# Loading wq in two transfers: sixteen rows first, then the other 112

## The chip, the cores and the metric

The kernel runs on one core of a Trainium2 chip. The metric is device time in microseconds for one execution. Six kinds of engine matter here: TensorE (PE, matrix products), VectorE (DVE), ScalarE (ACT), GpSimd (POOL), SyncE (SP, which here only issues transfers) and the sixteen DMA engines of the core, which move data from device memory (HBM) into the on-chip memory (SBUF, 128 rows called partitions).

## The reference

One decode step of a block with two branches, mixed by a scalar gate, all in float32:

```python
g = sigmoid((x * gate_w).sum(-1))                 # x: 1 x 1 x 512
q = (x @ wq).reshape(32 heads, 128)               # wq: 512 x 4096
scores = q . k_cache * 128 ** -0.5                # k_cache, v_cache: 8 heads x 32768 x 128
a = (softmax(scores) . v_cache).reshape(4096) @ wo     # four query heads share one k/v head
b = (silu(x @ w1) * (x @ w3)) @ w2                # 512 -> 1792 -> 512
out = g * a + (1 - g) * b
```

The two caches are 134 MB each; all inputs together are 296 MB, read once.

## The kernel before, in words

The program is written out by hand. `Program.add` takes one operation for one engine with the names of what it reads and writes, and works out from these names which semaphores the engine must wait for; `emit` then writes every engine's list in the order of adding.

All bulk transfers are added with `load` (its transfer is line 194 of the profile) on the queue of SyncE. SyncE works through its list in order: it waits until the buffer of the next load is free, issues it and goes on. Each load gets one of nine semaphores in turn (`lanes`), and a load waits for the one nine places before it. Value tiles are issued by a sister of `load` at line 413, on the same queue.

There are two large buffers, `big[0]` ("big_a") and `big[1]` ("big_b"), each 128 rows of 64 KB, 8.4 MB. Their halves have the names A0, A1 and B0, B1 in the bookkeeping. A key tile, a value tile or all of wq fills one buffer exactly.

The order at the start is:

- ACT issues two small transfers, x and gate_w, one row of 2 KB each, on its own queue (line 202).
- SP issues wq into `big[0]`, as one transfer of 128 rows. Row p holds rows 4p to 4p+3 of wq, 64 KB in one piece, both in HBM and in SBUF.
- SP issues the first key tile into `big[1]`.
- POOL and DVE prepare constants. TensorE turns x into a column (line 253), DVE copies it to `xp`.
- TensorE computes q from `xp` and wq (`part`, line 268: four groups of eight products, each 32 x 512), then a small product for the gate (line 279).
- SP may now issue the second key tile into `big[0]`, in place of wq.
- ACT and DVE bring q into the form in which it is used as weights (`win`, `winc`, lines 286 to 296).

After that comes a loop over sixteen key tiles (`scores`: DVE transposes pieces at line 346, TensorE multiplies them at line 330, ACT moves the part that has to leave the buffer into `aside` at line 318), four of which make up one softmax over a pair of k/v heads. Four tiles behind it run the value tiles (`values_loop`, TensorE at line 432). Key and value loads alternate on the queue. w1 and w3 are loaded on the way. At the end come the last value tiles (line 587), wo, and w2 in five pieces (products at lines 660 and 676), a copy (line 688) and the store (line 485).

Of the kernel before, what the change touches and what calls it, by code (L numbers as in the profile page):

```python
# [13 lines left out]
P = 128  # L14
# [102 lines left out]
def kernel(  # L117
# [19 lines left out]
    NC = D // P  # L137
# [18 lines left out]
    pe, dve, act, pool = (  # L156
        lambda fn, _e=e, **kw: pr.add(_e, fn, **kw) for e in ("PE", "DVE", "ACT", "POOL")
    )
    V, A, T = nc.vector, nc.scalar, nc.tensor

    def sbuf(name, *shape):
        return nc.alloc_sbuf_tensor(name, [P, *shape], F32)[:]

    big = [sbuf("big_a", 2 * R), sbuf("big_b", 2 * R)]
# [25 lines left out]
    def load(dst, src, writes, over=()):  # L190
        lanes[0] += 1
        lane = f"load{lanes[0] % 9}"
        return pr.add(
            "SP", lambda: nc.sync.dma_start(dst, src), writes=writes, over=[*over, lane], inc=lane, by=16, also=lane,  # L194
        )

    def region(b, z):
        return big[b][:, z * R:(z + 1) * R]


    for i, t in enumerate((x.rearrange("a b n -> (a b) n"), gate_w.rearrange("(o n) -> o n", o=1))):
        pr.add("ACT", lambda i=i, t=t: nc.scalar.dma_start(rows[i][0:1, :], t), writes=[f"row{i}"], inc="row", by=16)
    load(big[0], wq.rearrange("(p c) n -> p (c n)", c=NC), ["A0", "A1"])


    ident, ones, fold = sbuf("ident", P), sbuf("ones", P), sbuf("fold", 32)
# [1 line left out]
    spot, mask, xp = sbuf("spot", 16, 8), sbuf("mask", 16), sbuf("xp", NC, 32)  # L208
# [16 lines left out]
    for src, dst, view, axes in (  # L225
# [11 lines left out]
            reads=[src], writes=[dst])  # L237
# [24 lines left out]
    for c in range(NC):  # L262
        def part(c=c):
            t = region(0, c // 2)
            for b in range(2):
                for j in range(4):
                    o = ((c % 2) * HKV + 4 * b + j) * REP * DH
                    ins = T.matmul(  # L268
                        pf[b][32 * j:32 * j + 32, :], xp[:, c, :], t[:, o:o + REP * DH],
                        start=(c == 0), stop=(c == NC - 1),  # L270
                    )
            return ins
        pe(part, reads=["A0", "A1", "xp"], writes=["f0", "f1"])


    gpr, gsm = tmp[0:1, 1].rearrange("p b d -> p (b d)"), sbuf("gsm", 1)
# [5 lines left out]
        reads=["gate0"], writes=["gate1"])  # L282
# [414 lines left out]
    a, b, c, d = flips  # L697
# [67 lines left out]
```

## Time and profile before

| | |
|---|---|
| median of 3 runs | 694.1 us (693.98 to 695.0) |
| the profiled execution | 693.89 us, its span 692.1 us |
| mean granted TensorE clock | 0.802 of full speed |
| busy: PE, DVE, ACT, POOL | 56%, 53%, 19%, 0% of the span |
| read from HBM | 296.23 MB, 428 GB/s over the span |
| transfers of SP's queue | 99.1% of the time of 16 DMA engines |

The span runs from the first to the last instruction; the profiled execution's own time is 1.8 us longer. "SPq" and "ACTq" are the instruction queues of SyncE and ScalarE, where transfers are issued. A transfer's issue is short; its data moves later, in order behind what the queue already holds. In an engine row of the timeline the first number is the start in us, the second how long, and in brackets stands how long the engine was idle before and what ended that. In rows of windows, DMA share is the busy share of the sixteen DMA engines in that stretch; it can exceed 1 by a few hundredths because a packet is counted where it starts.

### The profile page before, as it was taken

The page shows a single profiled execution, that of the slowest core. Times are in us where ns is not written, and L with a number is a line of the kernel's source. Part 1 is how long each engine was busy: PE and PEld are TensorE (multiplying, and loading weights), DVE is VectorE, ACT ScalarE, POOL GpSimd, SP SyncE. Part 2 cuts the span into 40 slices and gives each one's busy share as a digit, 9 for nine tenths or more (in the row PEclk, how much of TensorE's full clock was granted, in tenths as well). Part 3 has the DMA queues.
Part 4 walks back from the last instruction along what each step waited for, and adds up shares of the span by engine and source line. Part 5 has one row for each costly group of instructions (what it writes and reads, how often), then busy time and mean ns, then how long its engine had stood idle before and what let it go on. Part 6 is the DMA issues. An engine that isn't in the chain of part 4 may idle for free. (4 is left out here: it accounts for less than half of the span.)

```text
span 692.1 us, 5789 instructions
## 1 busy us (share of the span) xinstructions
PE 388.3 (56%) x2448; PEld 95.3 (14%) x2448; DVE 370.1 (53%) x259; ACT 134.7 (19%) x113; POOL 2.8 (0%) x15
## 2 busy tenths in 40 slices
PE   1537677566473636565564646364563646564457
PEld 0101111201010101201010101101010101211112
DVE  1049998493725637493826537492816547600701
ACT  0143323222303131220303131220303031100000
POOL 1000000000000000000000000000000000000000
PEclk9969999968686966778695779788697879865789
DMA  9999999999999999999999999999999999999996
GB/s 394 444 432 424 428 424 432 449 439 432 424 432 424 443 447 432 428 428 428 432 443 443 428 428 428 428 443 447 432 424 428 428 436 439 421 451 425 422 429 287
DMA packets 6213, 296.35 MB, mean 428 GB/s; under 512 B 694, under 2 KB 698, under 8 KB 1084
## 3 DMA queue, kind: packets, MB, share of 16 engines
q1 hardware_dynamic: 6196, 296.23, 99.1%
q8 instruction: 6, 0.10, 0.1%
q14 instruction: 3, 0.02, 0.0%
q10 hardware_dynamic: 8, 0.01, 0.0%
HBM read 296.23 MB, written 0.00 MB: 428 GB/s over the span
## 5 line engine op out<-in xcount | busy, mean ns | idle before, releaser
L346 DVE STREAM_TRANSPOSE aside<-big_a 128x2048 f32<-128x2048 f32 x41 | 94.4, 2302 | 184.3 <-DMA big_a<-in_A_k_cache_dram 184.3
L330 PE MATMUL ps<-aside,winc 128*32 128x512 f32 x512 | 89.4, 776 | 168.0 <-PEq L703 167.2
L330 PE MATMUL ps<-kt,winc 128*32 128x512 f32 x512 | 89.0, 772 | 49.1 <-PEq L703 49.1
L318 ACT COPY aside<-big_a 128x6144 f32<-128x6144 f32 x14 | 74.4, 5313 | 171.2 <-DMA big_a<-in_A_k_cache_dram 171.2
L432 PE MATMUL ps<-big_b,pv 128*32 128x512 f32 x768 | 94.9, 650 | 17.4 <-PEq L703 17.4
L346 DVE STREAM_TRANSPOSE kt<-aside 128x2048 f32<-128x2048 f32 x32 | 72.7, 2273 | 0.0
L346 DVE STREAM_TRANSPOSE kt<-big_a 128x2048 f32<-128x2048 f32 x28 | 63.5, 2269 | 0.0
L330 PEld LDWEIGHTS ps<-aside,winc 128*32 128x32 f32 x512 | 13.1, 120 | 236.6 <-issue 236.6
L358 ACT COPY sb<-ps 128x512 f32<-128x512 f32 x16 | 17.1, 1071 | 136.5 <-PE ps L330 136.5
L432 PEld LDWEIGHTS ps<-big_b,pv 128*32 128x32 f32 x768 | 27.7, 119 | 85.0 <-issue 85.0
L346 DVE STREAM_TRANSPOSE aside<-aside 128x2048 f32<-128x2048 f32 x16 | 36.3, 2269 | 0.0
L587 PE MATMUL ps<-big_b,probs 128*32 128x512 f32 x128 | 19.1, 756 | 21.1 <-DMA big_b<-in_A_v_cache_dram 21.1
L330 PEld LDWEIGHTS ps<-kt,winc 128*32 128x32 f32 x512 | 13.1, 120 | 125.4 <-issue 125.4
L596 DVE TENSOR_SCALAR red<-ps,own_b 128x128 f32<-128x128 f32 x2 | 0.7, 350 | 52.7 <-PE ps L587 52.7
L324 ACT COPY winc<-win 128x128 f32<-128x128 f32 x32 | 9.8, 307 | 77.9 <-PE ps L330 77.9
L587 PE MATMUL ps<-big_a,probs 128*32 128x512 f32 x128 | 18.1, 730 | 7.6 <-DMA big_a<-in_A_v_cache_dram 7.6
L346 DVE STREAM_TRANSPOSE aside<-big_b 128x2048 f32<-128x2048 f32 x7 | 16.0, 2291 | 11.0 <-DMA big_b<-in_A_k_cache_dram 11.0
L641 PE MATMUL ps<-win,ones 128*128 128x512 f32 (+1 forms) x40 | 21.8, 631 | 0.0
L242 PE MATMUL ps<-acc 128*128 128x512 f32 x34 | 20.0, 670 | 2.5 <-POOL acc L213 1.5
L379 DVE TENSOR_REDUCE mt<-turned 128x8 f32<-128x2048 f32 x4 | 9.2, 2292 | 20.3 <-PE turned L368 20.3
L405 DVE TENSOR_REDUCE sums<-probs 128x8 f32<-128x2048 f32 x4 | 15.3, 3834 | 2.1 <-ACT probs L398 2.1
L268 PE MATMUL turned<-big_a,xp 128*32 128x512 f32 x64 | 8.6, 699 | 12.0 <-DMA big_a<-in_A_wq_dram 12.0
(94 smaller groups left out, 186.9 us busy)
## 6 DMA issues: line engine op xcount, KB each, us to landing
big_b<-in_A_v_cache_dram SPq DMA_DIRECT2D x2, 4096.0 KB, 25.8
big_b<-in_B_w_dram SPq DMA_DIRECT2D x2, 3584.0 KB, 20.8
aside<-in_A_wo_dram SPq DMA_DIRECT2D x1, 4096.0 KB, 29.4
big_a<-in_A_wo_dram SPq DMA_DIRECT2D x1, 4096.0 KB, 20.4
big_a<-in_B_w_dram SPq DMA_DIRECT2D x2, 1024.0 KB, 23.5
big_a<-in_B_w_dram SPq DMA_DIRECT2D x1, 768.0 KB, 26.0
big_a<-in_B_w_dram SPq DMA_DIRECT2D x1, 512.0 KB, 26.7
big_a<-in_B_w_dram SPq DMA_DIRECT2D x1, 256.0 KB, 26.9
```

The source lines that it names most:

```text
L242: return T.matmul(ps_s, acc[:, 0:P], acc, start=True, stop=False, skip_group_check=True)
L268: ins = T.matmul(pf[b][32 * j:32 * j + 32, :], xp[:, c, :], t[:, o:o + REP * DH], start=(c == 0), stop=(c == NC - 1),)
L318: act(lambda: A.copy(spare, src[:, :, 32:128]), reads=[key], writes=["wo"])
L324: lambda: A.copy(winc, win[:, t // 4, :, 16 - 16 * z:48 - 16 * z]),
L330: ins = T.matmul(ps_s[32 * g:32 * g + 32, :], winc[:, c, :], kt[c % 2][:, 512 * g:512 * g + 512], start=False, stop=False, skip_group_chec ...
L346: k = dve(lambda d=dst, s=src: V.transpose(d, s), reads=[key], writes=[f"kt{c % 2}"], credit="keys")
L358: lambda: A.copy(sb[:, :, :, t % 4], ps_s.rearrange("p (n i) -> p n i", i=32)),
L379: dve(lambda: V.tensor_reduce(mt[:, 0:8], turned.rearrange("p (n q) -> p q n", q=8), axis=AX.X, op=ALU.max), reads=banks, writes=["mt"])
L405: dve(lambda: V.tensor_reduce(sums[:, 8 * w:8 * w + 8].rearrange("p (u q) -> p u q", u=2), probs[:, :, 0:1024].rearrange("p u (n q) -> p u ...
L432: ins = T.matmul(ps_o[32 * t:32 * t + 32, :], pv[:, o:o + 32], big[1][:, n * P:(n + 4) * P], start=((z, g) == (0, 0)), stop=((z, g) == (1, ...
L587: ins = T.matmul(ps_o[32 * t:32 * t + 32, :], prob[u][:, o:o + 32], vt[:, n * P:(n + 4) * P], start=((e, z, g) == (0, 0, 0)), stop=((e, z, ...
L641: return T.matmul(bank[:, 0:n], ones, win.rearrange("p w c n -> p (w c n)")[:, 0:n], start=True, stop=True)
```

## The change

The transfer of wq is split by rows. The first covers rows 0 to 15 of the buffer (1 MB), the second rows 16 to 127 (7.3 MB). Both are issued by SP, one after the other, ahead of the first key tile. The first has a name of its own, "wq", for the bookkeeping, and the q product waits for both. Every later load takes the next of the nine semaphores.

```diff
-    load(big[0], wq.rearrange("(p c) n -> p (c n)", c=NC), ["A0", "A1"])
+    wqd = wq.rearrange("(p c) n -> p (c n)", c=NC)
+    load(big[0][0:16], wqd[0:16], ["wq"])
+    load(big[0][16:P], wqd[16:P], ["A0", "A1"])
...
-        pe(part, reads=["A0", "A1", "xp"], writes=["f0", "f1"])
+        pe(part, reads=["A0", "A1", "wq", "xp"], writes=["f0", "f1"])
```

Two lines are added, so line numbers behind them are higher by two in the changed kernel (the q product's matmuls stand at line 270).

## The prediction

> **What bounds the kernel now.** I read the page from the top: engine shares, the forty slices, the queue list. Then the stretches by window for the start, the chain of waits for the end, and the timeline for the first 45 us.
>
> ```profile
> span 692.1 us, 5789 instructions
> PE 388.3 (56%) x2448; PEld 95.3 (14%) x2448; DVE 370.1 (53%) x259; ACT 134.7 (19%) x113; POOL 2.8 (0%) x15
> DMA  9999999999999999999999999999999999999996
> GB/s 394 444 432 424 428 424 432 449 439 432 424 432 424 443 447 432 428 428 428 432 443 443 428 428 428 428 443 447 432 424 428 428 436 439 421 451 425 422 429 287
> q1 hardware_dynamic: 6196, 296.23, 99.1%
> ```
>
> No engine is busy for much more than half of the span; the DMA row is 9 in every slice but the last. The queue line carries most of the argument: q1 is the queue of the SP engine, all loads go through it, and its packets fill 99.1% of what sixteen DMA engines have in 692.1 us. That leaves 0.9%, 6.2 us. The next rows show where these 6.2 us are.
>
> ```profile
> core 0: us, PE busy (x) PEld busy (x) DVE busy (x) ACT busy (x) POOL busy (x), PEclk, DMA share, GB/s
> 0.00:2.00 2.00, 0.46 (x1) 0.46 (x2) 0.00 (x0) 0.22 (x1) 1.02 (x7) 1.00 0.49 165
> 2.00:12.00 10.00, 2.22 (x6) 0.59 (x5) 2.45 (x10) 1.06 (x1) 1.79 (x8) 1.00 0.94 387
> 12.00:24.00 12.00, 0.99 (x8) 0.40 (x12) 0.48 (x1) 0.00 (x0) 0.00 (x0) 1.00 1.01 437
> ...
> 120.00:240.00 120.00, 69.65 (x444) 16.13 (x444) 68.97 (x44) 28.19 (x23) 0.00 (x0) 0.77 1.00 433
> 688.00:692.00 4.00, 1.24 (x32) 0.53 (x24) 0.29 (x1) 0.00 (x0) 0.00 (x0) 0.97 0.03 10
> ```
>
> The DMA engines are half empty for the first 2 us, a little short until 12 us, empty for the last 4 us, and full between. So there is no gap later on in which a late start could be made good. What the first transfers lose is lost at the end, unless the compute was itself waiting for something else; the chain says it was not.
>
> ```profile
> 661.57 26.71 DMA big_a<-in_B_w_dram
> 688.27 0.04 issue
> 688.32 1.10 PE turned L676 x24
> 689.42 0.02 issue
> 689.44 0.29 DVE winc L688
> ```
>
> The chain ends on a transfer that was 26.71 us on its way, almost all of it behind other data; after the last landing come 1.10 us of matmuls, a copy of 0.29 us and the store. The profiled execution took 693.89 us, 1.8 more than its span; the median of the three runs is 694.1, 0.2 above it.
>
> **The unit of the sum.** One row of wq in this layout is 64 KB (four rows of 4096 floats). From the queue line, one DMA engine moves 296.23 MB / (16 x 692.1 us x 0.991) = 27.0 GB/s while busy, so one row takes one engine 2.43 us. I call that a slot. A load of 128 rows is eight slots on each of sixteen engines, 19.4 us. The timeline agrees with that:
>
> ```profile
> 0.93 0.40 SPq L194 DMA_DIRECT2D big_a<-in_A_wq_dram  x1
> 1.39 0.41 SPq L194 DMA_DIRECT2D big_b<-in_A_k_cache_dram  x1
> 23.01 8.62 PE L268 MATMUL turned<-big_a,xp 128*32 128x512 f32 x64 [12.02 <-DMA big_a<-in_A_wq_dram]
> 31.56 0.38 PE L279 MATMUL ps<-gsm,ones 1*128 1x1 f32 x2
> 31.69 0.33 SPq L194 DMA_DIRECT2D big_a<-in_A_k_cache_dram  x1
> 43.30 2.31 DVE L346 STREAM_TRANSPOSE aside<-big_b 128x2048 f32<-128x2048 f32 x1 [9.34 <-DMA big_b<-in_A_k_cache_dram]
> ```
>
> wq is used at 23.01, the first key tile at 43.30: 20.3 us apart.
>
> **The change, part by part.** *One more issue on SP.* The wq issue takes 0.40 us; a second one pushes the first key load from 1.39 to about 1.8. Cost nothing: that load stands behind wq's 19.4 us of data anyhow. Without that cover it would be 0.4 us.
>
> *One more completion.* Another transfer posts its own completion on each engine. The page counts them with the small packets:
>
> ```profile
> DMA packets 6213, 296.35 MB, mean 428 GB/s; under 512 B 694, under 2 KB 698, under 8 KB 1084
> ```
>
> All 694 together cannot cost more than the 6.2 us that are not data, so 16 more cost at most 0.14 us. I take nothing.
>
> *One more wait on TensorE.* The q product (line 268) now waits for two landings. Queued behind it on TensorE are its own 64 matmuls, the gate product of line 279 and the whole loop; and the second key load on SP waits for line 279, since it overwrites wq's buffer. The first piece lands before the second, so the wait itself is free. If wq as a whole lands late by d, the second key load is issued at 31.69 + d, and the first key tile, behind wq on every engine, lands at about 43.30 + d. The 11.6 us between them, in which the queue still has work, stay as they are. No new hole, but no gain either.
>
> *The waits for loads nine places back* move by one number. The loads they name landed long before; cost nothing. The x and gate rows on ACT's queue pass between wq's packets and may come later than before:
>
> ```profile
> 10.38 0.61 PE L253 MATMUL ps<-ident,probs 1*128 1x1 f32 x4 [6.76 <-DMA probs<-in_gate_w_dram]
> ```
>
> They are used at 10.38 and needed by 23.01, so 12 us of cover hide it.
>
> *The shape of the two transfers.* This is the term that decides. The trace holds no bulk load of fewer than 128 rows, so it must be bounded from both sides.
>
> Low end: only the DMA engines limit the pace. Sixteen rows are one slot on each engine, 112 are seven; eight as before, cost 0.
>
> High end: the rows on the SBUF side limit it, each accepting its share of the pace and no more. 437 GB/s over 128 rows is 3.4 GB/s a row, and a 64 KB row takes 19.2 us however few rows go along. Then each of the two transfers lasts as long as the whole one did: sixteen slots for eight, +8 x 2.43 = +19.4 us.
>
> [...] Twelve slots from below and the sixteen of the high end from above give +9.7 to +19.4 us; I take the middle, fourteen slots, **+6 x 2.43 = 14.6 us**.
>
> [...]
>
> [...]
>
> **The sum.** 693.9 + 14.6 = 708.5 us against the profiled execution; the median stands 0.2 above it, so 708.7. This case alone spans twelve to sixteen slots: 703.6 to 713.3, or to 715 with some disorder in the start.
>
> **The rivals.**
>
> *Nothing happens.* The engines are the only limit and both pieces spread evenly: 694.1, with the small terms 694.2 to 694.7. For it: q1 is a single queue that runs full, and each engine gets one row and then seven, exactly the old eight. Against it: it needs SBUF to accept sixteen rows at the pace of 128. Chance 0.14.
>
> *Uneven spread over engines only.* 112 rows are given out eight to an engine, as 128 were, on fourteen engines; with the first row that is nine slots, +2.4 us, 696.5. Nothing in the trace speaks on it. Chance 0.05.
>
> *A worse order.* [...] Chance 0.04.
>
> *Faster.* [...] The place is the first 12 us. At 437 GB/s the 165 of the first 2 us are worth 0.76 us, so 1.24 are missing, 0.93 of them before the issue that the change cannot move; the 387 of the next ten are 1.14 us short. 0.31 + 1.14 = 1.45 us at most: 692.6. It decides only if narrow pieces run at the full pace. The wq issue itself, 0.40 us, is the part most likely to shrink. Chance of passing the bound below: 0.05. [...]
>
> **How the numbers follow.** Narrow pieces lose time as summed: 0.72. A difference of 0.2%, 1.4 us, is about what a measurement of this kernel can tell from none. Slower by more than that are the forecast, the uneven spread and the worse order, 0.72 + 0.05 + 0.04 = 0.81; the same 0.14; faster 0.05. Leaving out the worse order, the gain and some tail, the range runs from the no-effect case at 693.8 to 715.
>
> **What would show it.** In the profile after: two wq issues, at 0.9 and about 1.4 us; the q product starting at about 23 + 14.6 = 37.6 us instead of 23.01; a GB/s figure of the first slice well under 394, about 108 GB/s (1 MB in four slots) over the first 10 us; the first key tile used near 58; every later event shifted by one constant, the 4 us at the end unchanged. If the first 1 MB arrives slowly and the rest at full pace, twelve slots hold; if also the stretch from 10 to 35 us is under 437, more. If the q product starts within 1 us of 23.01, the forecast is wrong and the engines alone set the pace. If it starts late but the end does not move, my claim that nothing later can absorb it is wrong.

## The result, and the profile after

The changed kernel takes 714.6 us (median of 5 runs, 713.98 to 715.76) where the kernel before takes 694.1 (5 runs, 693.85 to 695.0): ratio 1.0298, 95% interval 1.0283 to 1.0312, 20.5 us slower. The profiled execution took 715.64 us, 1.0 above that median, with a span of 713.5, 21.4 us longer than the span before.

The page after, its engines, slices and main queue:

```profile
span 713.5 us, 5790 instructions
PE 388.4 (54%) x2448; PEld 96.5 (14%) x2448; DVE 370.0 (52%) x259; ACT 134.7 (19%) x113; POOL 2.8 (0%) x15
DMA  9999999999999999999999999999999999999996
GB/s 177 235 345 460 419 422 427 444 424 448 426 437 437 426 441 426 426 448 426 441 434 426 441 426 426 449 422 445 430 430 441 422 430 448 411 450 434 416 433 263
q1 hardware_dynamic: 6212, 296.23, 99.0%
```

Engine times and bytes are those of before. The busy share of the DMA engines is too: 99.0% against 99.1%, with a 9 in the very first slice. Only the rate has changed, and only in three slices: 177, 235 and 345 GB/s, where 394, 444 and 432 stood. From the fourth slice on the two rows look alike. So the busy share hides the loss completely: the engines are occupied by packets that move slowly (below: 8.64 us for the first rows, where 2.42 is normal). The rows by window show the stage; a packet is counted where it starts, so with long packets a short window can overshoot, here by up to 0.20:

```profile
0.00:2.00 2.00, 0.46 (x1) 0.47 (x2) 0.00 (x0) 0.22 (x1) 1.02 (x8) 1.00 1.05 132
2.00:12.00 10.00, 1.61 (x2) 0.04 (x1) 1.51 (x7) 1.06 (x1) 1.79 (x8) 1.00 1.20 184
12.00:24.00 12.00, 0.61 (x4) 0.55 (x4) 1.42 (x3) 0.00 (x0) 0.00 (x0) 1.00 0.84 224
24.00:44.00 20.00, 0.00 (x0) 0.00 (x0) 0.00 (x0) 0.00 (x0) 0.00 (x0) 1.00 0.93 233
44.00:65.00 21.00, 8.94 (x66) 2.69 (x66) 2.53 (x4) 5.93 (x21) 0.00 (x0) 0.84 1.02 441
```

About half the pace or less until 44 us, then 441. The timeline gives the shift of each step:

```profile
0.92 0.86 SPq L194 DMA_DIRECT2D big_a<-in_A_wq_dram  x2
1.83 0.47 SPq L194 DMA_DIRECT2D big_b<-in_A_k_cache_dram  x1
12.51 0.61 PE L255 MATMUL ps<-ident,probs 1*128 1x1 f32 x4 [8.90 <-DMA probs<-in_gate_w_dram]
44.67 8.63 PE L270 MATMUL turned<-big_a,xp 128*32 128x512 f32 x64 [31.55 <-issue]
53.36 0.35 SPq L194 DMA_DIRECT2D big_a<-in_A_k_cache_dram  x1
63.93 2.31 DVE L348 STREAM_TRANSPOSE aside<-big_b 128x2048 f32<-128x2048 f32 x1 [8.30 <-DMA big_b<-in_A_k_cache_dram]
```

The q product starts at 44.67 instead of 23.01 (its row names no transfer as what ended the wait, but the last packets of wq end at 43.5 us). The second key load is issued 21.7 us later, the first key tile is used 20.6 us later. The chain of waits at the end is the old one, shifted:

```profile
683.14 26.58 DMA big_a<-in_B_w_dram
709.72 0.04 issue
709.76 1.11 PE turned L678 x24
710.87 0.02 issue
710.89 0.29 DVE winc L690
```

709.76 instead of 688.32: 21.4 us. Nothing between the first 45 us and the end gave any of it back. Taken in the order of their ends, the bulk packets of the queue are 20.0 to 21.1 us later than before almost all the way; only the last few are up to 21.5 later, in an execution 1.0 us above the median.

The trace's packet records say how it happened. Nearly every data packet at the start is one 64 KB row, moved by one engine. Sorted by start and taken sixteen at a time (so that a group is about one row of each engine), their median durations are, in us:

```
                         row 1  row 2  row 3  row 4  row 5  row 6  row 7  row 8 | key tile
before                    3.17   2.42   2.42   2.42   2.42   2.42   2.42   2.42 | 2.42
after (1 row + 7 rows)    8.64   5.36   4.76   2.99   3.62   4.59   4.76   4.47 | 3.18, then 2.42
```

The first piece's row takes 8.64 us, the seven rows of the second piece sum to 30.55. Together 39.2, where before had 20.1: 19.1 us, and 0.8 more on the first row of the key tile. Against before, the first piece is 5.5 us over one row (8.64 - 3.17) and the second 13.6 us over seven (30.55 - 16.94).

### The profile page after: what moved, and what is told of

Read it like the earlier page. It is cut to its first block, busy times and chain, and to the rows that moved or that the text cites. A ratio compares the mean times of both kernels' runs of the same rounds, so it can differ in the third digit from the quotient of the medians.

```text
span 713.5 us, 5790 instructions
## 1 busy us (share of the span) xinstructions
PE 388.4 (54%) x2448; PEld 96.5 (14%) x2448; DVE 370.0 (52%) x259; ACT 134.7 (19%) x113; POOL 2.8 (0%) x15
## 3 DMA queue, kind: packets, MB, share of 16 engines
q1 hardware_dynamic: 6212, 296.23, 99.0%
## 5 line engine op out<-in xcount | busy, mean ns | idle before, releaser
L589 PE MATMUL ps<-big_b,probs 128*32 128x512 f32 x128 | 18.3, 730 | 19.4 <-DMA big_b<-in_A_v_cache_dram 19.4
L348 DVE STREAM_TRANSPOSE aside<-big_b 128x2048 f32<-128x2048 f32 x7 | 16.1, 2297 | 10.4 <-DMA big_b<-in_A_k_cache_dram 10.0
L283 DVE TENSOR_SCALAR gate<-gate 128x1 f32<-128x1 f32 x1 | 0.2, 153 | 39.2 <-ACT gate L282 39.2
```

The source lines that it names most:

```text
L348: k = dve(lambda d=dst, s=src: V.transpose(d, s), reads=[key], writes=[f"kt{c % 2}"], credit="keys")
L589: ins = T.matmul(ps_o[32 * t:32 * t + 32, :], prob[u][:, o:o + 32], vt[:, n * P:(n + 4) * P], start=((e, z, g) == (0, 0, 0)), stop=((e, z, ...
```

## The experiments

The theory on trial, an assumption of the author: rows on the SBUF side share entrances in groups, and a transfer whose rows lie in few entrances holds up all sixteen engines. No record shows an entrance; the runs can only say whether the times fit. The rivals: any second transfer at the start costs this; the slow side is HBM; one of the two pieces alone is to blame. In every kernel below the q product waits for all pieces of wq. The code shown leaves out the lists of names that say so; three dots stand for them.

**Is it the second transfer, or the narrow shape?** Split by columns instead of rows.

```diff
-    load(big[0][0:16], wqd[0:16], ["wq"])
-    load(big[0][16:P], wqd[16:P], ["A0", "A1"])
+    load(big[0][:, 0:2048], wqd[:, 0:2048], ["wq"])
+    load(big[0][:, 2048:], wqd[:, 2048:], ["A0", "A1"])
...
```

> wq is split by columns: the first transfer brings 8 KB of every one of the 128 rows, the second the other 56 KB, same queue and same waits. Theory of narrow transfers (rows on the SBUF side share entrances, a transfer of few neighbouring rows finds too few of them): both pieces are 128 rows wide, so nothing is lost, 694 us within 1.5. Rival of the second transfer (another issue, another landing to wait for, another completion): the whole loss stays, about 714 us.

Measured: 694.05 us, ratio to before 0.9999 (0.999 to 1.0009). The split itself is free: two issues, two landings, the completions of a second transfer (16 more packets on the main queue in the changed kernel, 6212 against 6196), the same lane shift. The timeline of the column split:

```profile
0.92 0.88 SPq L194 DMA_DIRECT2D big_a<-in_A_wq_dram  x2
1.85 0.45 SPq L194 DMA_DIRECT2D big_b<-in_A_k_cache_dram  x1
31.75 0.33 SPq L194 DMA_DIRECT2D big_a<-in_A_k_cache_dram  x1
```

The SP queue does at the start what it does in the changed kernel, and the second key load is issued at 31.75, as before (31.69). The rival of the second transfer is out.

**Does a sixteen-row piece stay slow?** All of wq in such pieces.

```diff
-    load(big[0][0:16], wqd[0:16], ["wq"])
-    load(big[0][16:P], wqd[16:P], ["A0", "A1"])
+    parts_wq = [f"wq{j}" for j in range(7)]
+    for j in range(8):
+        load(big[0][16 * j:16 * j + 16], wqd[16 * j:16 * j + 16], ["A0", "A1"] if j == 7 else [f"wq{j}"])
...
```

> wq in eight transfers of 16 neighbouring rows. In the changed kernel the first such piece ran for about 9 us where 2.4 were its share. Theory of narrow transfers: each of the eight takes four slots of 2.43 us, 32 instead of 8, so 694 + 58 = 752 us, and about 108 GB/s for the first 75 us. Rival that the first piece was slow because it was the first (a cold start): later pieces run at full pace, about 701 us.

Measured: 749.3 us, ratio 1.0794 (1.0773 to 1.0816), 55 us slower where 58 were expected. Two windows of this kernel:

```profile
24.00:44.00 20.00, 0.00 (x0) 0.00 (x0) 0.00 (x0) 0.00 (x0) 0.00 (x0) 1.00 0.94 105
44.00:65.00 21.00, 0.00 (x0) 0.00 (x0) 0.00 (x0) 0.00 (x0) 0.00 (x0) 1.00 0.90 100
```

105 and 100 GB/s where 437 is normal, about a quarter, with engines 90 to 94% busy, and not only at the start: a cold start is out.

**Rows eight apart.** In this kernel and the next two the loop above stays, with another choice of rows.

```diff
-        load(big[0][16 * j:16 * j + 16], wqd[16 * j:16 * j + 16], ...)
+        load(big[0][j:P:8], wqd[j:P:8], ...)
```

> wq in eight transfers of 16 rows again, but row j, j+8, j+16 and so on: sixteen rows eight apart, in HBM as in SBUF. Theory of narrow transfers, with entrances shared by four neighbours and nothing else: no two rows of a piece are neighbours, nothing is lost, 694 to 696 us. [...] Rival that sixteen-row transfers are slow wherever the rows lie: 752 us.

Measured: 716.4 us, ratio 1.032 (1.0299 to 1.0341). Not the 694 of "only neighbours share", and not 749 either. From 11 to 41 us the kernel moves 210 GB/s, and by the packet records a row takes 5.1 us, about twice the normal 2.42. In the terms of the theory an entrance would then serve rows that are far apart, too; which rows, and how many, the times don't say.

**HBM or SBUF?** Rows eight apart at one end, neighbours at the other.

```diff
+        load(big[0][16 * j:16 * j + 16], wqd[j:P:8], ...)      # from eight apart, to neighbours
+        load(big[0][j:P:8], wqd[16 * j:16 * j + 16], ...)      # the other kernel: the reverse
```

> Eight transfers of 16 rows that read rows eight apart in HBM and write 16 neighbouring rows of SBUF (so wq's rows end up permuted and q is another; the work is the same). It separates the two ends of the transfer, which moved together so far. Theory of narrow transfers (the SBUF side decides): as with neighbours at both ends, 749 us. Rival that the HBM side decides (16 neighbouring rows of 64 KB read at once): as with rows eight apart at both ends, 716 us.

> The other way round: eight transfers of 16 rows that read neighbouring rows of HBM and write SBUF rows eight apart (wq's rows are permuted again). Narrow transfers on the SBUF side: 716 us. Rival of the HBM side: 749 us.

Measured: 748.4 us when SBUF gets neighbours (1.0779, 1.0757 to 1.0801), 715.4 when SBUF gets rows eight apart (1.0304, 1.0283 to 1.0325). The same window, first of the kernel that writes neighbours, then of the one that writes rows eight apart:

```profile
24.00:44.00 20.00, 0.00 (x0) 0.00 (x0) 0.00 (x0) 0.00 (x0) 0.00 (x0) 1.00 0.93 105
```

```profile
24.00:44.00 20.00, 0.00 (x0) 0.00 (x0) 0.00 (x0) 0.00 (x0) 0.00 (x0) 1.00 0.92 210
```

105 belongs to neighbours in SBUF, 210 to rows eight apart there, whatever HBM sees. For pieces of sixteen rows the limit is on the SBUF side; this is shown, not only argued.

**Halves.**

```diff
-    load(big[0][0:16], wqd[0:16], ["wq"])
-    load(big[0][16:P], wqd[16:P], ["A0", "A1"])
+    for j in range(2):
+        load(big[0][64 * j:64 * j + 64], wqd[64 * j:64 * j + 64], ["A0", "A1"] if j == 1 else [f"wq{j}"])
...
```

> wq in two transfers of 64 neighbouring rows. Theory of narrow transfers: with four rows to an entrance 64 rows reach sixteen entrances, and nothing is lost, 694 us; with eight rows to an entrance, spread so that 64 neighbours meet only half of them, each piece takes as long as a whole load, 713.5 us. Rival that the loss goes with the number of rows outside of full loads of 128 by engine count alone (64 rows are four to each engine, evenly): 694 us.

Measured: 715.4 us, ratio 1.0306 (1.0285 to 1.0327). By count four rows to each engine, evenly, and still a loss of 21.3 us: even counts on the engines don't help. The packet records have 5.1 us a row, as with sixteen rows eight apart, and the rate from 11 to 41 us is 210 GB/s in both. In the terms of the theory 64 neighbours would find half of the entrances that 128 rows find; this is inferred from the time alone.

**How are the 112 rows dealt out?** The second piece imitated by seven of sixteen rows.

```diff
     load(big[0][0:16], wqd[0:16], ["wq"])
-    load(big[0][16:P], wqd[16:P], ["A0", "A1"])
+    for j in range(7):
+        load(big[0][16 + j:P:7], wqd[16 + j:P:7], ["A0", "A1"] if j == 6 else [f"wq{j}"])
...
```

> The first sixteen rows as in the changed kernel, the other 112 in seven transfers of 16 rows, seven apart: piece j has rows 16+j, 23+j, 30+j and so on. If the 112-row transfer gives each engine a block of seven neighbouring rows, this is the same work in the same order, and the time is that of the changed kernel, 714.6 us within 2. If it deals rows out in turn (16 neighbours at a time), the changed kernel would have had seven rounds of 9.4 us, which its 44.67 us for the start of the q product rules out; if in some other order, this kernel differs from 714.6 by more than 2.

Measured: 714.9 us, ratio 1.0297 (1.0276 to 1.0317), the changed kernel's time. The packet records agree row by row:

```
                    row 1  row 2  row 3  row 4  row 5  row 6  row 7  row 8
after                8.64   5.36   4.76   2.99   3.62   4.59   4.76   4.47
seven apart          8.98   5.31   4.65   2.94   3.67   4.41   4.58   4.40
```

So the times fit engines that each get a block of seven neighbouring rows and work through it in order; the records don't name the engine. At every step the sixteen rows in flight are then about seven apart, and some steps are slower (4.8 us) than others (3.0). In no step is any engine spared: the quickest of the sixteen rows took 2.81 to 5.07 us in the changed kernel, where 2.42 is the normal time. Which end of the transfer holds up rows that are seven apart was not tried by itself; in this kernel they are seven apart at both ends.

**What does each piece cost by itself?** wq whole, in one transfer, and an additional transfer ahead of it, 32 KB of each row, into a free buffer: 16 rows, or 112, or for comparison all 128.

```diff
-    load(big[0][0:16], wqd[0:16], ["wq"])
-    load(big[0][16:P], wqd[16:P], ["A0", "A1"])
+    parts_wq = ["more"]
+    load(pool_w[0:16], wqd[0:16, 0:8192], ["more"])            # or [16:P], or all rows
+    load(big[0], wqd, ["A0", "A1"])
...
```

> wq whole again, in one transfer of 128 rows; ahead of it an additional transfer of 16 neighbouring rows, 32 KB of each (0.5 MB), into a buffer that is still free, and the q product waits for it too. It gives the price of the small piece by itself, at half its size. Narrow transfers: 0.5 MB at the 111 GB/s that sixteen-row pieces reached is 4.7 us, 698.8 us. Rival that the small piece is cheap and the whole loss is that of the 112 rows: 0.5 MB at 437 GB/s is 1.2 us, 695.3 us.

> The counterpart: wq whole, and ahead of it an additional transfer of the 112 rows from 16 on, 32 KB of each (3.7 MB). In the changed kernel seven rows of 64 KB per engine took from about 11 to about 41.5 us, 30.5 us, where an even spread takes 17. Narrow transfers: half of it, 15.2 us on top of 694.1, 709.3 us, or a little less where engines that are done early go on with their part of the whole load. Rival that the 112 rows run at full pace: 3.7 MB at 437 GB/s, 8.4 us, 702.5 us.

> The measure for the two additions: all 128 rows, 32 KB of each (4.2 MB), loaded ahead of the whole wq. Narrow transfers: this one is not narrow, so its price is its bytes, 4.2 MB at 437 GB/s or 9.6 us, 703.7 us: less than the additional 112 rows cost, although it brings more. Rival that any additional transfer at the start is dear: as much above its bytes as the 112 rows.

Measured: with 16 rows 698.74 us (1.0064, 1.0047 to 1.0081), with 112 rows 708.23 (1.0206, 1.0188 to 1.0223), with 128 rows 703.91 (1.0148, 1.0131 to 1.0165). The dearest is not the one with the most bytes: 112 rows cost 14.2 us, 128 rows 9.8. The issue rows of the first two kernels (KB, then us to landing) show the additional piece alone:

```profile
aside<-in_A_wq_dram SPq DMA_DIRECT2D x1, 512.0 KB, 6.9
```

```profile
aside<-in_A_wq_dram SPq DMA_DIRECT2D x1, 3584.0 KB, 16.7
```

At 437 GB/s the 0.5 MB would be worth 1.2 us and the 3.7 MB 8.4 us. Above that the 16 rows cost 4.5 - 1.2 = 3.3 us and the 112 rows 14.2 - 8.4 = 5.8 us, at half size. Twice that is 6.7 and 11.5 us: both pieces are to blame, the large one more. They add up to 18.2 of the 20.5 us; the rest is left open. (The packet records of the changed kernel itself divide it as 5.5 and 13.6 us.)

**The other order.** Rows 0 to 111 first, the last sixteen after them.

```diff
-    load(big[0][0:16], wqd[0:16], ["wq"])
-    load(big[0][16:P], wqd[16:P], ["A0", "A1"])
+    load(big[0][0:112], wqd[0:112], ["wq"])
+    load(big[0][112:P], wqd[112:P], ["A0", "A1"])
...
```

> The same two sizes in the other order: rows 0 to 111 first, rows 112 to 127 after them. Narrow transfers: the same few entrances, so about the same loss, 714 us within 3 (the last sixteen rows meet their entrances while some engines are already loading the first key tile, which may take a little off or add it). Rival that a narrow piece is dear only while nothing else is under way at the start: 707 us or less.

Measured: 715.07 us, ratio 1.0304 (1.0283 to 1.0324). It does not matter which piece is first; the last sixteen rows' packets have a median of 8.43 us.

## Why the prediction was right, and where its size was off

*The bound and the shift.* Right: the DMA queue is the limit throughout (99.0% of the time of sixteen engines), and what the first transfers lose is lost at the end (21.7 us at the second key load, 21.4 at the last landing).

*The small terms.* Right, and the column split shows them together at nothing: the issue on SP (the key load's went from 1.39 to 1.83, 1.8 foretold), the completions (711 small packets instead of 694), the wait on TensorE, the loads nine places back. The gate row came at 12.51 instead of 10.38, long before 44.67. The bound on the completions was set in the wrong place: 690 of the 694 packets are on the main queue, so their time lies inside its 99.1% and not in the 6.2 us outside it. At a median of 9 ns each they cost nothing all the same. One detail was wrong: the 11.6 us between the second key load's issue and the first key tile's use shrank to 10.6 (53.36 to 63.93), since the q product waits for the slowest engine of wq (43.5 us by the packet records) while the first (41.0 us) are already loading the tile. It costs nothing.

*The mechanism.* Right in kind, as far as the runs go: transfers of 16, 64 or 112 rows load more slowly than one of 128, and the two kernels with different rows at the two ends (748.4 and 715.4 us) show that for pieces of sixteen rows it is the SBUF side that decides. A 64 KB row takes 5.1 us in the sixteens eight apart and in the halves, and 9.3 to 9.4 us in the sixteens of neighbours, where 2.42 is normal: factors of about two, two and four. Groups of rows that share an entrance to SBUF would give such factors, but no run shows how many entrances there are or which rows share one. For the 112 rows sharing is argued from these factors; the runs do not show that it gives their size, as the next paragraphs say.

*The size of the term.* 14.6 us foretold, 20.5 measured: 14 slots foretold, and by the packet rows 39.2 / 2.43 = 16.1, against 8.3 before: 7.9 slots lost, not six. No run shows the twelve slots at the lower end of the sum, nor the four for the first piece; in their place the changed kernel showed 3.6 slots for the first piece (8.64 us) and 12.6 for the second (30.55 us). The step that was mis-sized is the second piece, for which the middle was taken, ten slots, as the half-way point between an even spread and the high end. The middle assumed that only some rows are held up; in the records all of them are, at every step: none took less than 2.81 us.

*What sets the size of the second piece.* The first piece ran at 121 GB/s (1.05 MB in 8.64 us). The seven steps of the second are not alike: rows 4 and 5 of the packet table took 2.99 and 3.62 us, the other five 4.47 to 5.36. In the kernel that loads rows 0 to 111 first, the fourth and fifth of its seven steps are the two quickest: 3.49 and 3.50 us, where the other five have 4.20 to 4.76. So the time of a step seems to go with the rows that are in flight. Yet even the quickest steps are above 2.42 us, so something holds up every row. Neither is explained by a run, and with it part of the size of the larger piece stays open.

*The high end was no end.* Sixteen slots, +19.4 us, were given as the most that rows with a pace of their own could cost. The changed kernel lies at 20.5, and the halves, which at two slots for each row would stand exactly there, at 21.3: a row took 5.1 us there, and not 4.86. So the own range of the narrow case, 703.6 to 713.3, missed the time; the "some disorder in the start", which brought it to 715, was a guess that happened to cover it. That 714.6 lies inside the stated range, by 0.4 us, is luck. Eight pieces of 16 rows also show that 19.4 us is not the price of *a* narrow row but of its company: with the pace fixed for each row, eight such pieces would have cost eight whole loads, 136 us more, and they cost 55.

*The rivals.* No effect and faster are out by the result; the uneven spread over engines is out by its price, 2.4 us where 20.5 were lost, and the halves, which are even, lose as much (21.3). The worse order, the 112 rows dealt out in turn, sixteen neighbours at a time, is out by the q product's start at 44.67 us, since seven rounds of 9.4 us would have ended far later. For a kernel that is built so, the price was nearly right: 752 expected, 749.3 measured with eight sixteens.

## What to carry to other kernels

Split a load by columns, not by rows: here pieces that keep all 128 rows cost nothing extra (8 and 56 KB of each row: 694.05 us against 694.1), while in a piece of 16 neighbours, of 64 or of 112 rows every row was held up (8.4 to 9.4, 5.1 and on average 4.4 us, where 2.42 is normal, for rows of 64 KB), and on a queue that is never empty the whole delay reached the end (21.7 us at the second key load, 21.4 at the last landing). When a DMA-bound profile gets slower at the same bytes, look at the GB/s row and at the duration of single packets and not at the busy share: here the queue's share of the span stood at 99.0%, although the rate was at about half of the normal 437 GB/s or less for the first 44 us, and with eight sixteens the engines were 90 to 94% busy at a quarter of it. And a bound should say what it holds fixed; "as slow as one row alone", 19.4 us, was not the worst case here, where 20.5 and 21.3 were measured.

## What the runs showed of the hardware that was not expected

The time of a row does not simply double and double again. One 64 KB row takes 2.42 us where all 128 rows are loaded: 27.1 GB/s. In the halves and the sixteens eight apart a row takes 5.1 us, so two rows together get 25.7 GB/s, 5% less. In the sixteens of neighbours a row takes 9.3 to 9.4 us, so four rows together get 27.9 to 28.2 GB/s, a little more. (That two and four rows share an entrance there is inferred from the factors, since the records don't name the entrance.) Why two together do worse than four was not tried.

That a transfer of 112 rows is given out in blocks of seven neighbouring rows, engine by engine, could be inferred from time alone, by building the same order out of other transfers: 714.9 us against 714.6, and row by row within 0.34 us. The records don't name the engine.
